# Gate logits with column tiles over quarters of the tokens, and VectorE's transpose to put them on token rows

## The chip, the cores and the metric

The kernel runs on one core of one Trainium2 chip. The metric is the device time of one execution in microseconds. The kernel before takes 374.43 us, the median of three runs (373.29 to 374.58).

Five engines matter: TensorE multiplies matrices (PE in the profile, PEld its weight loads), VectorE (DVE) and ScalarE (ACT) work on elements, GpSimd (POOL) adds tiles and issues the large loads, and SyncE (SP) issues transfers. SBUF is the working memory of 128 partitions; PSUM is the memory that TensorE writes.

## The reference, cut to what matters

An attention is followed by a mixture of experts with a gate in two stages. The gate is what the change touches: for each of 3072 tokens (8 batches of 384), 4 group logits and 4 expert logits of the chosen group.

```python
q: (8, 16, 384, 64)   k, v: (8, 4, 384, 64)
x = attention(q, k, v)                     # 3072 tokens x 1024
g_logits = x @ w_group                     # 1024 x 4
g_idx = argmax(g_logits)                   # and its softmax weight g_w
e_logits = x[g_idx == g] @ w_expert[g]     # 1024 x 4 for each of 4 groups
e_idx = argmax(e_logits)                   # and its softmax weight e_w
h  = maximum(x @ w1[g, e], 0)              # 1024 x 1024
ye = h @ w2[g, e]                          # 1024 x 1024
out = (g_w * e_w) * ye
```

The kernel computes all 4 + 16 = 20 logits of every token in one product with a matrix `wg` of 20 columns, padded to 32.

## The kernel before

It goes batch by batch; a "block" is one batch `b`, with its attention followed by the experts' products of the batch before it. The weights of one expert per batch are fetched early, by a guess: the mean of the next batch's `v` is put through the gate before its attention is done.

The parts that matter (`KQ` = 8 pieces of 128 of the 1024 features, `S` = 384 tokens, `SC` = 3 pieces of 128 tokens, `NW` = 20 logits; cuts are marked with `...`):

```python
def ps_tile(which, ...):        # PSUM: two tiles of two banks "s", two "o", taken in turn;
    ...                         # "x" is the "o" tile that is not the current one

# gate logits: 4 column tiles of 32 columns; each sums its own 2 of the 8 feature pieces
def gate_logits(b, pt):
    lg = pt[:, 0]
    for jj in range(KQ // 4):
        for t in range(4):
            kq = 4 * jj + t
            nc.tensor.matmul(out=lg[32 * t:32 * t + 32, :S], lhsT=wg[:, kq, :],
                             rhs=xT[b][:, kq, :],
                             start=(jj == 0), stop=(jj == KQ // 4 - 1))
    ls = gpool.tile([P, S], F32, name="lgs")
    nc.scalar.copy(out=ls, in_=lg[:, :S])
    lgs[b] = ls

# sums the four partial logits (mod32 has ones where row % 32 == column), tokens come to rows
def gate_tokens(b, glp):
    for c in range(SC):
        nc.tensor.matmul(out=glp[:, c, :], lhsT=lgs[b][:, c * P:(c + 1) * P],
                         rhs=mod32[:, 0, :NW], start=True, stop=True)

def guess_mean(b, pt): ...      # 12 small matmuls: mean of v, into pt[:, 1, :4]
def guess_logits(vm, glp): ...  # 4 small matmuls: the guess's logits, beside the tokens' logits

def gate_softmax(b, glp, guess, eng=None):
    ...
    evac(eng or nc.vector, gl, glp[:, lo:hi])      # one copy out of PSUM
    ...                                            # 9 small VectorE operations: both argmaxes

# the experts' products
def ffn_h(x, w1, hT, f0, which, mid=None):   # w1, two of eight pieces; then ReLU on ScalarE
    ...
def ffn_y(w2, hT, c, which, nhs=(0, 1), y=None, fs=None):   # w2, one of three token pieces
    ...

def block(b):
    f = b - 1
    prefetch(b)      # GpSimd: waits for the next batch's transposed q, then fetches w1, w2
    moe_h(f, 0, "s")
    ...
    sums(b, 0, Hkv, "o")
    for m in range(4):
        normalise(b, m)                      # xT, the gate's input
    ...
    moe_y(f, 0, "s")
    ...
    y = ffn_y(w2s[f], hTs[f], 1, "s", (0,))
    gate_logits(b, ps_tile("o"))
    ffn_y(w2s[f], hTs[f], 1, "s", (1,), y)
    y_out(f, 1, y)
    pt = ps_tile("s")
    glp = gate_rows(pt)
    gate_tokens(b, glp)
    if not last:
        guess_mean(b + 1, pt)
        vm = mean_copy(pt, nc.vector)
    y = ffn_y(w2s[f], hTs[f], 2, "o", (0,))
    if not last:
        guess_logits(vm, glp)
    weights[b] = gate_softmax(b, glp, not last)
    if not last:
        pick_index(b + 1)
        at[b + 1] = Attn(b + 1)
        y_scores(f, at[b + 1], y)            # rest of the third output piece, first scores
        return {}
    ...

def prefetch(b):
    if b != 2:
        pick(b)
    if b + 1 < B:
        transposed(b + 1)                    # GpSimd reads one column of the transposed q
    pick_w1(b)                               # 2 MB as bf16, cast on the way
    pick_w2(b)                               # the same
    if b + 2 < B:
        loads(b + 2)                         # v, k and q of the batch after the next
```

After the last block TensorE does the eighth batch's `ffn_h` (all of w1) and `ffn_y` (all of w2), and the results are written out. Blocks 0 and 1 have the same steps in a schedule of their own.

Of the kernel before, what the change touches and what calls it, by code (L numbers as in the profile page):

```python
# [9 lines left out]
F32 = mybir.dt.float32  # L10
# [8 lines left out]
def kernel(  # L19
# [416 lines left out]

    lgs = {}

    def gate_logits(b, pt):
        lg = pt[:, 0]
        for jj in range(KQ // 4):
            for t in range(4):
                kq = 4 * jj + t
                nc.tensor.matmul(out=lg[32 * t:32 * t + 32, :S], lhsT=wg[:, kq, :],  # L446
                                 rhs=xT[b][:, kq, :],
                                 start=(jj == 0), stop=(jj == KQ // 4 - 1))
        ls = gpool.tile([P, S], F32, name="lgs")
        nc.scalar.copy(out=ls, in_=lg[:, :S])  # L450
        lgs[b] = ls

    def guess_mean(b, pt):

# [13 lines left out]
    def gate_rows(pt):  # L468
        return pt[:, 1, 64:64 + (SC + 1) * NW].rearrange("p (c n) -> p c n", n=NW)

    def gate_tokens(b, glp):
        for c in range(SC):
            nc.tensor.matmul(out=glp[:, c, :], lhsT=lgs[b][:, c * P:(c + 1) * P],  # L473
                             rhs=mod32[:, 0, :NW], start=True, stop=True)

    def guess_logits(vm, glp):
        for g in range(Hkv):
            nc.tensor.matmul(out=glp[:, SC, :], lhsT=vm[:, g:g + 1].to_broadcast([P, P]),  # L478
                             rhs=wgd[:, g, :], start=(g == 0), stop=(g == Hkv - 1))

    def gate_softmax(b, glp, guess, eng=None):

        lo = 0 if b is not None else SC
        hi = SC + 1 if guess else SC
        n, nt = hi - lo, SC - lo
        gl = gpool.tile([P, SC + 1, NW], F32, name="gl")[:, lo:hi]
        evac(eng or nc.vector, gl, glp[:, lo:hi])
        mx = gpool.tile([P, 2, SC + 1], F32, name="mx")[:, :, lo:hi]
        nc.vector.tensor_reduce(out=mx[:, 0, :], in_=gl[:, :, :G], axis=AX.X, op=ALU.max)
        sh = gpool.tile([P, 2, SC + 1, G], F32, name="sh")[:, :, lo:hi]  # L490
# [3 lines left out]
        ohg = gpool.tile([P, SC + 1, G], F32, name="ohg")[:, lo:hi]  # L494
        nc.vector.tensor_single_scalar(ohg, sh[:, 0], 0.0, op=ALU.is_ge)
        pr = gpool.tile([P, SC + 1, G, Eg], F32, name="pr")[:, lo:hi]
        nc.vector.tensor_tensor(out=pr, in0=gl[:, :, G:].rearrange("p c (g e) -> p c g e", g=G),
                                in1=ohg.unsqueeze(3).to_broadcast([P, n, G, Eg]), op=ALU.mult)
        el = gpool.tile([P, SC + 1, Eg], F32, name="el")[:, lo:hi]
# [6 lines left out]
        ohe = gpool.tile([P, SC + 1, Eg], F32, name="ohe")[:, lo:hi]  # L506
        nc.vector.tensor_single_scalar(ohe, sh[:, 1], 0.0, op=ALU.is_ge)
        oh = oh_all[:, b, lo:hi] if b is not None else oh_first.unsqueeze(1)
        nc.vector.tensor_tensor(out=oh.rearrange("p c (g e) -> p c g e", g=G),
                                in0=ohg.unsqueeze(3).to_broadcast([P, n, G, Eg]),  # L510
                                in1=ohe.unsqueeze(2).to_broadcast([P, n, G, Eg]), op=ALU.mult)

        def weights():
            ex = gpool.tile([P, 2, SC, G], F32, name="ex")
            nc.scalar.activation(ex, sh[:, :, :nt], ACT.Exp)
# [9 lines left out]
    def first_choice(glp):  # L525

        gl = glp[:, SC, :]
# [155 lines left out]
        state["vm"] = mean_copy(state["pt"], nc.scalar)  # L683

    def first_pick():
        glp = gate_rows(state["pt"])
        guess_logits(state["vm"], glp)
        first_choice(glp)
        pick_index(0)

    def first_fetch():
# [61 lines left out]
    guess_mean(1, pt)  # L753
    vm = mean_copy(pt, nc.scalar)
    moe_h(0, 2, "s", do(sums, 1, 0, 2, "s"))
    glp = gate_rows(pt)
    gate_tokens(0, glp)
    guess_logits(vm, glp)
    for m in range(2):
        normalise(1, m)  # L760
    moe_h(0, 4, "s")
    weights[0] = gate_softmax(0, glp, True, nc.scalar)
    pick_index(1)
    moe_h(0, 6, "s")
    nc.sync.dma_start(out=xb_dram[0], in_=xb[0])
# [2 lines left out]
    def first_block():  # L768

        prefetch(1)  # L770
        collect(1, 2, Hkv)
        weights[0]()
        out_weights(0)
        cast(1, 0)
        cast(1, 1)
        moe_y(0, 0, "s")
        sums(1, 2, Hkv, "o")
        normalise(1, 2)
        normalise(1, 3)
        moe_y(0, 1, "s")  # L780
        cast(1, 2)
        cast(1, 3)
        nc.sync.dma_start(out=xb_dram[1], in_=xb[1])
        y = ffn_y(w2s[0], hTs[0], 2, "o", (0,))
        gt = ps_tile("x")
        guess_mean(2, gt)
        gate_logits(1, gt)
        state["vm"] = mean_copy(gt, nc.vector)
        at[2] = Attn(2)

        def second_gate():
            glp = gate_rows(gt)
            gate_tokens(1, glp)
            guess_logits(state["vm"], glp)
            weights[1] = gate_softmax(1, glp, True)
            pick_index(2)
            pick(2)

        y_scores(0, at[2], y, second_gate)
        return {}  # L800

# [10 lines left out]
    def block(b):  # L812
# [17 lines left out]
        cast(b, 3)  # L830
        nc.sync.dma_start(out=xb_dram[b], in_=xb[b])
        y = ffn_y(w2s[f], hTs[f], 1, "s", (0,))
        gate_logits(b, ps_tile("o"))
        ffn_y(w2s[f], hTs[f], 1, "s", (1,), y)
        y_out(f, 1, y)
        pt = ps_tile("s")
        glp = gate_rows(pt)
        gate_tokens(b, glp)
        if not last:
            guess_mean(b + 1, pt)  # L840
            vm = mean_copy(pt, nc.vector)
# [133 lines left out]
```

The softmax here doesn't subtract the row's maximum and nothing guards it: scores larger than these inputs give would overflow.

## Time and profile before

| | us |
|---|---|
| time, median of 3 | 374.43 |
| span of the profiled execution | 372.4 |
| TensorE busy | 361.1 |
| VectorE busy | 258.1 |
| ScalarE busy | 233.0 |
| GpSimd busy | 150.6 |

The lines that touch the gate, from the costliest groups with the shapes kept apart. The columns are: line, engine, operation, output <- inputs, shapes, count, then the busy time in us and the mean ns of one, then the engine's idle time before them and what ended it:

```profile
L446 PE MATMUL ps_o<-xT,wg 128*32 128x384 f32 x112 | 10.5, 492 | 0.0
...
L473 PEld LDWEIGHTS ps_s<-mod,lgs 128*128 128x128 f32 x36 | 5.0, 191 | 0.9
L473 PE MATMUL ps_s<-mod,lgs 128*128 128x20 f32 x36 | 4.4, 252 | 0.0
...
L450 ACT COPY lgs<-ps_o 128x384 f32<-128x384 f32 x8 | 3.8, 479 | 5.3 <-PE ps_o L446 5.3
```

L446 is `gate_logits`, L473 `gate_tokens`, L450 the copy between them, L460 `guess_mean`, L478 `guess_logits`, L305 and L324 the attention's two products, L611 `ffn_h`, L622 `ffn_y`. An fp32 matmul appears as two records, one for each pass. "128*32" is the part of the array that an instruction uses. The durations of matmuls overlap, so what one costs is read from where the next one starts, not from its own duration. A few matmul records are missing from the trace.

### The profile page before, as it was taken

The numbers are of one execution on the slowest core, as the hardware profiler recorded it, in microseconds if no ns is written. First come the engines' busy times: TensorE is split into PE (matmuls) and PEld (weight loads), VectorE is DVE, ScalarE is ACT, GpSimd is POOL, SyncE is SP. The second block draws the span as 40 slices with busy tenths as digits, with TensorE's granted clock in tenths as the row PEclk, the third lists the DMA queues.
The fourth block names the chain that finished last, engine by engine and source line by source line (L and its number), as shares of the span: only waits on it lengthen the run. The fifth ranks groups of instructions, "written<-read, shape, count | busy, mean of one in ns | idle before, by whom it ended". The sixth has DMA issues, their size and how long they took to land.

```text
span 372.4 us, 8914 instructions
## 1 busy us (share of the span) xinstructions
PE 361.1 (97%) x3648; PEld 183.8 (49%) x3663; DVE 258.1 (69%) x491; ACT 233.0 (63%) x309; POOL 150.6 (40%) x118
## 2 busy tenths in 40 slices
PE   8999999999999999999999999999999999999992
PEld 3545446445454545544555445544545445554641
DVE  5699787858976498737989189764897379892230
ACT  4789943759926597367954599265972679544221
POOL 6666950706804176033730367113760237500000
PEclk9999999999999999999999999999999999999997
DMA  8986999999999999999999999989999999999734
GB/s 189 242 108 101 241 213 156 234 239 281 222 152 184 249 263 210 147 195 291 238 208 153 255 246 216 199 167 246 264 212 150 203 212 238 196 201 234 238 73 99
DMA packets 71209, 76.02 MB, mean 204 GB/s; under 512 B 35928, under 2 KB 50264, under 8 KB 71168
## 3 DMA queue, kind: packets, MB, share of 16 engines
q0 software_dynamic: 26640, 41.03, 63.0%
q1 hardware_dynamic: 44096, 33.81, 37.1%
q8 instruction: 29, 0.48, 0.5%
q10 hardware_dynamic: 432, 0.61, 0.5%
q14 instruction: 12, 0.10, 0.1%
HBM read 89.21 MB, written 18.87 MB: 290 GB/s over the span
## 4 chain that ended last, share of the span: by engine, by line
PE 91%; DVE 3%; ACT 2%; issue 1%; POOL 1%; ACTq 0%; POOLq 0%
PE ps_o L324 29%; PE ps_s L611 21%; PE ps_s L622 14%; PE ps_s L305 8%; PE ps_o L622 8%; PE ps_o L446 3%; PE ps_o L268 2%; DVE red L338 1%; PE ps_o L611 1%; PE ps_o L408 1%; ACT e L311 1%; PE ps_s L473 1%; DVE ps_o L419 1%; DVE xT L428 1%; POOL e L331 1%
## 5 line engine op out<-in xcount | busy, mean ns | idle before, releaser
L311 ACT ACTIVATE e<-ps_s 128x768 f32<-128x768 f32 x192 | 150.3, 814 | 22.1 <-PE ps_s L305 19.3
L324 PE MATMUL ps_o<-e,v_raw 64*64 64x384 f32 x1536 | 153.1, 482 | 0.2 <-DVE xT L428 0.2
L331 POOL TENSOR_TENSOR e<-e 128x768 f32<-128x768 f32 x64 | 116.1, 1832 | 88.6 <-ACT e L311 64.6
L338 DVE TRANSPOSE_TENSOR_REDUCE red<-e 128x24 f32<-128x768 f32 x128 | 114.3, 947 | 11.9 <-POOL e L331 11.9
L611 PE MATMUL ps_s<-xb,w 128*128 128x384 bf16 x480 | 81.1, 326 | 0.4 <-ACT hT L615 0.2
L324 PEld LDWEIGHTS ps_o<-e,v_raw 64*64 64x64 f32 x1536 | 55.4, 133 | 37.5 <-issue 27.1
L611 PEld LDWEIGHTS <-w 128*128 128x128 bf16 x512 | 48.9, 98 | 36.1 <-issue 3.9
L305 PE MATMUL ps_s<-qT,kT 64*64 64x384 bf16 x768 | 63.7, 326 | 0.4 <-ACT e L311 0.2
L615 ACT ACTIVATE hT<-ps_s 128x768 bf16<-128x768 f32 x30 | 24.3, 810 | 61.0 <-PE ps_s L611 61.0
L622 PEld LDWEIGHTS <-hT 128*128 128x128 bf16 x384 | 35.5, 98 | 45.1 <-issue 6.5
L622 PE MATMUL ps_s<-w,hT 128*128 128x512 bf16 x240 | 56.0, 379 | 0.4
L305 PEld LDWEIGHTS <-kT 64*64 64x64 bf16 x768 | 24.3, 105 | 38.4 <-issue 36.7
L678 POOL COPY after<-qT 128x1 bf16<-128x1 bf16 x7 | 2.1, 301 | 79.8 <-DMA qT<-q_raw 76.9
L622 PE MATMUL ps_o<-w,hT 128*128 128x512 bf16 x129 | 31.1, 379 | 0.6 <-issue 0.2
L419 DVE STREAM_TRANSPOSE rb<-inv 128x384 f32<-128x384 f32 x60 | 31.0, 555 | 0.3
L647 ACT ACTIVATE ot<-ps_s,we 128x1024 f32<-128x1024 f32 x14 | 15.6, 1114 | 19.1 <-PE ps_s L622 19.1
L428 DVE TENSOR_TENSOR xT<-xT,rb 128x768 f32<-128x768 f32 x25 | 24.0, 958 | 0.9
L242 DVE CAST vm<-ps_s 128x4 bf16<-128x4 f32 x5 | 0.8, 163 | 29.8 <-PE ps_s L460 29.8
L240 ACT CAST xb<-xT 128x768 bf16<-128x768 f32 x27 | 21.1, 827 | 0.0
L374 DVE COPY xT<-ps_o 128x768 f32<-128x768 f32 x18 | 16.5, 919 | 0.0
L376 ACT COPY xT<-ps_o 128x768 f32<-128x768 f32 x10 | 8.0, 801 | 6.5 <-PE ps_o L324 6.5
L242 DVE COPY gl<-ps_s 128x80 f32<-128x80 f32 (+1 forms) x6 | 1.4, 239 | 14.0 <-PE ps_s L478 8.4
(132 smaller groups left out, 196.8 us busy)
## 6 DMA issues: line engine op xcount, KB each, us to landing
w<-in_moe_w_dram POOLq DMA_DIRECT2D x16, 2048.0 KB, 21.8
out_dram<-ot SPq DMA_DIRECT2D x42, 256.0 KB, 7.1
xb_scratch<-xb SPq DMA_DIRECT2D x8, 768.0 KB, 9.6
q_raw<-in_q_dram POOLq DMA_DIRECT2D x7, 768.0 KB, 33.7
v_raw<-in_v_dram SPq DMA_DIRECT2D x14, 384.0 KB, 5.6
out_dram<-ot SPq DMA_DIRECT2D x11, 128.0 KB, 2.3
k<-in_k_dram POOLq DMA_DIRECT2D x7, 192.0 KB, 30.5
w<-in_q_dram POOLq DMA_DIRECT2D x3, 192.0 KB, 6.7
```

The lines of the kernel that those rows point to most:

```text
L240: eng.copy(out=out_, in_=in_)
L305: nc.tensor.matmul(out=sT[r * H2:(r + 1) * H2, s, :S], lhsT=kT[b][s * D:(s + 1) * D, slot, ks], rhs=qT[b][s * D:(s + 1) * D, kq * SC:(kq + ...
L311: nc.scalar.activation(e.rearrange("p t (s x) -> p s t x", s=2), sT[:, :, :S].rearrange("p s (t x) -> p s t x", t=2), ACT.Exp, scale=scale)
L324: nc.tensor.matmul(out=oT[t * D:(t + 1) * D, r, :S], lhsT=vraw[b][r * H2:(r + 1) * H2, g, c * D:(c + 1) * D], rhs=self.e[u][r * H2:(r + 1) ...
L331: eng.tensor_add(out=self.e[u], in0=self.e[u], in1=self.e[u + 1])
L338: nc.vector.tensor_reduce(out=reds[self.b][:, g, n].rearrange("p t j -> p (t j)"), in_=self.e[u].rearrange("p t (j x) -> p (t j) x", x=32) ...
L374: nc.vector.tensor_copy(out=dst, in_=src)
L419: nc.vector.transpose(out=rb[:, r].rearrange("p (j x) -> p j x", x=32), in_=inv[b][:, 2 * m + r].unsqueeze(2).to_broadcast([P, NB, 32]))
L428: eng.tensor_mul(out=x, in0=x, in1=rb)
L611: nc.tensor.matmul(out=h[:, jj, :S], lhsT=w1[:, kq, (f0 + jj) * P:(f0 + jj + 1) * P], rhs=x[:, kq, :], start=(kq == 0), stop=(kq == KQ - 1))
L615: nc.scalar.activation(hT[:, f0:f0 + 2, :], h[:, :, :S], ACT.Relu)
L622: nc.tensor.matmul(out=y[:, nh, :], lhsT=hT[:, f, c * P:(c + 1) * P], rhs=w2[:, f, nh * HALF:(nh + 1) * HALF], start=(f == 0), stop=(f == ...
```

## The change

Before, the four column tiles split the features: each sums a quarter of x, for all tokens, and a second product on TensorE adds the four parts and turns the result so that tokens lie on rows. After, the four column tiles split the tokens: column tile `t` takes tokens 32t to 32t + 31 of each piece of 128, and sums all of x in place, in PSUM. The second product and the copy before it are no longer needed. VectorE's transpose of 32x32 blocks turns each block where it stands, which puts every token on its own row. It aims at less work on TensorE and ScalarE in each block, and one PSUM tile less.

The logits are now 32 matmuls of 96 columns instead of 8 of 384, and the small products of the guess move up: `guess_mean` right behind the logits, in the same PSUM tile, `guess_logits` and the softmax ahead of the third output piece. The core of the diff (cut: the softmax's views for a case that no longer occurs, and renamed arguments):

```diff
     def gate_logits(b, pt):
-        lg = pt[:, 0]
-        for jj in range(KQ // 4):
+        for kq in range(KQ):
+            x = xT[b][:, kq, :].rearrange("p (c t i) -> p t c i", t=4, i=32)
             for t in range(4):
-                kq = 4 * jj + t
-                nc.tensor.matmul(out=lg[32 * t:32 * t + 32, :S], lhsT=wg[:, kq, :],
-                                 rhs=xT[b][:, kq, :],
-                                 start=(jj == 0), stop=(jj == KQ // 4 - 1))
-        ls = gpool.tile([P, S], F32, name="lgs")
-        nc.scalar.copy(out=ls, in_=lg[:, :S])
-        lgs[b] = ls
+                nc.tensor.matmul(out=pt[32 * t:32 * t + 32, 0, :32 * SC], lhsT=wg[:, kq, :],
+                                 rhs=x[:, t], start=(kq == 0), stop=(kq == KQ - 1))
-    def gate_tokens(b, glp):
-        for c in range(SC):
-            nc.tensor.matmul(out=glp[:, c, :], lhsT=lgs[b][:, c * P:(c + 1) * P],
-                             rhs=mod32[:, 0, :NW], start=True, stop=True)
...
     def gate_softmax(b, pt, guess):
-        evac(eng or nc.vector, gl, glp[:, lo:hi])
+        gl = gpool.tile([P, SC + 1, 32], F32, name="gl")
+        nc.vector.transpose(out=gl[:, :SC], in_=pt[:, 0, :32 * SC].rearrange("p (c i) -> p c i", i=32))
+        if guess:
+            nc.vector.tensor_copy(out=gl[:, SC, :NW], in_=guess_row(pt))
...
 # block 0
-    glp = gate_rows(pt)
-    gate_tokens(0, glp)
-    guess_logits(vm, glp)
+    guess_logits(vm, pt)
...
 # block 1
         gt = ps_tile("x")
+        gate_logits(1, gt)
         guess_mean(2, gt)
-        gate_logits(1, gt)
         state["vm"] = mean_copy(gt, nc.vector)
...
 # blocks 2 to 7
-        gate_logits(b, ps_tile("o"))
-        ffn_y(w2s[f], hTs[f], 1, "s", (1,), y)
-        y_out(f, 1, y)
-        pt = ps_tile("s")
-        glp = gate_rows(pt)
-        gate_tokens(b, glp)
+        pt = ps_tile("o")
+        gate_logits(b, pt)
         if not last:
             guess_mean(b + 1, pt)
             vm = mean_copy(pt, nc.vector)
+        ffn_y(w2s[f], hTs[f], 1, "s", (1,), y)
+        y_out(f, 1, y)
+        if not last:
+            guess_logits(vm, pt)
+        weights[b] = gate_softmax(b, pt, not last)
         y = ffn_y(w2s[f], hTs[f], 2, "o", (0,))
-        if not last:
-            guess_logits(vm, glp)
-        weights[b] = gate_softmax(b, glp, not last)
```

More of the change, by code (lines that the diff above doesn't have):

```diff
@@ L435, in cast @@
         evac(eng or nc.scalar, xb[b][:, ks, :], xT[b][:, ks, :])
-    lgs = {}
     def gate_logits(b, pt):
-        lg = pt[:, 0]
-        for jj in range(KQ // 4):
+        for kq in range(KQ):
+            x = xT[b][:, kq, :].rearrange("p (c t i) -> p t c i", t=4, i=32)
             for t in range(4):
-                kq = 4 * jj + t
-                nc.tensor.matmul(out=lg[32 * t:32 * t + 32, :S], lhsT=wg[:, kq, :],
-                                 rhs=xT[b][:, kq, :],
-                                 start=(jj == 0), stop=(jj == KQ // 4 - 1))
-        ls = gpool.tile([P, S], F32, name="lgs")
-        nc.scalar.copy(out=ls, in_=lg[:, :S])
-        lgs[b] = ls
+                nc.tensor.matmul(out=pt[32 * t:32 * t + 32, 0, :32 * SC], lhsT=wg[:, kq, :],
+                                 rhs=x[:, t], start=(kq == 0), stop=(kq == KQ - 1))
     def guess_mean(b, pt):
@@ L466, in mean_copy, with guess_row, guess_logits, gate_softmax @@
         return vm
-    def gate_rows(pt):
-        return pt[:, 1, 64:64 + (SC + 1) * NW].rearrange("p (c n) -> p c n", n=NW)
-    def gate_tokens(b, glp):
-        for c in range(SC):
-            nc.tensor.matmul(out=glp[:, c, :], lhsT=lgs[b][:, c * P:(c + 1) * P],
-                             rhs=mod32[:, 0, :NW], start=True, stop=True)
-    def guess_logits(vm, glp):
+    def guess_row(pt):
+        return pt[:, 1, 64:64 + NW]
+    def guess_logits(vm, pt):
         for g in range(Hkv):
-            nc.tensor.matmul(out=glp[:, SC, :], lhsT=vm[:, g:g + 1].to_broadcast([P, P]),
+            nc.tensor.matmul(out=guess_row(pt), lhsT=vm[:, g:g + 1].to_broadcast([P, P]),
                              rhs=wgd[:, g, :], start=(g == 0), stop=(g == Hkv - 1))
[L481 to L486, printed above, removed]
-        evac(eng or nc.vector, gl, glp[:, lo:hi])
-        mx = gpool.tile([P, 2, SC + 1], F32, name="mx")[:, :, lo:hi]
+    def gate_softmax(b, pt, guess):
+        n = SC + 1 if guess else SC
+        gl = gpool.tile([P, SC + 1, 32], F32, name="gl")
+        nc.vector.transpose(out=gl[:, :SC], in_=pt[:, 0, :32 * SC].rearrange("p (c i) -> p c i", i=32))
+        if guess:
+            nc.vector.tensor_copy(out=gl[:, SC, :NW], in_=guess_row(pt))
+        gl = gl[:, :n, :NW]
+        mx = gpool.tile([P, 2, SC + 1], F32, name="mx")[:, :, :n]
         nc.vector.tensor_reduce(out=mx[:, 0, :], in_=gl[:, :, :G], axis=AX.X, op=ALU.max)
-        sh = gpool.tile([P, 2, SC + 1, G], F32, name="sh")[:, :, lo:hi]
+        sh = gpool.tile([P, 2, SC + 1, G], F32, name="sh")[:, :, :n]
         nc.vector.tensor_tensor(out=sh[:, 0], in0=gl[:, :, :G],
@@ L493, in gate_softmax @@
                                 op=ALU.subtract)
-        ohg = gpool.tile([P, SC + 1, G], F32, name="ohg")[:, lo:hi]
+        ohg = gpool.tile([P, SC + 1, G], F32, name="ohg")[:, :n]
         nc.vector.tensor_single_scalar(ohg, sh[:, 0], 0.0, op=ALU.is_ge)
-        pr = gpool.tile([P, SC + 1, G, Eg], F32, name="pr")[:, lo:hi]
+        pr = gpool.tile([P, SC + 1, G, Eg], F32, name="pr")[:, :n]
         nc.vector.tensor_tensor(out=pr, in0=gl[:, :, G:].rearrange("p c (g e) -> p c g e", g=G),
                                 in1=ohg.unsqueeze(3).to_broadcast([P, n, G, Eg]), op=ALU.mult)
-        el = gpool.tile([P, SC + 1, Eg], F32, name="el")[:, lo:hi]
+        el = gpool.tile([P, SC + 1, Eg], F32, name="el")[:, :n]
         nc.vector.tensor_reduce(out=el, in_=pr.rearrange("p c g e -> p c e g"), axis=AX.X,
@@ L505, in gate_softmax @@
                                 op=ALU.subtract)
-        ohe = gpool.tile([P, SC + 1, Eg], F32, name="ohe")[:, lo:hi]
+        ohe = gpool.tile([P, SC + 1, Eg], F32, name="ohe")[:, :n]
         nc.vector.tensor_single_scalar(ohe, sh[:, 1], 0.0, op=ALU.is_ge)
-        oh = oh_all[:, b, lo:hi] if b is not None else oh_first.unsqueeze(1)
+        oh = oh_all[:, b, :n]
         nc.vector.tensor_tensor(out=oh.rearrange("p c (g e) -> p c g e", g=G),
@@ L514, in weights @@
             ex = gpool.tile([P, 2, SC, G], F32, name="ex")
-            nc.scalar.activation(ex, sh[:, :, :nt], ACT.Exp)
+            nc.scalar.activation(ex, sh[:, :, :SC], ACT.Exp)
             sm = gpool.tile([P, 2, SC], F32, name="smx")
@@ L523, in gate_softmax, with first_choice @@
         return weights
-    def first_choice(glp):
-        gl = glp[:, SC, :]
+    def first_choice(gl):
         mx = gpool.tile([P, 2], F32, name="fmx")
@@ L685, in first_pick @@
     def first_pick():
-        glp = gate_rows(state["pt"])
-        guess_logits(state["vm"], glp)
-        first_choice(glp)
+        guess_logits(state["vm"], state["pt"])
+        first_choice(guess_row(state["pt"]))
         pick_index(0)
@@ L761 @@
     moe_h(0, 4, "s")
-    weights[0] = gate_softmax(0, glp, True, nc.scalar)
+    weights[0] = gate_softmax(0, pt, True)
     pick_index(1)
@@ L791, in second_gate @@
         def second_gate():
[L792 to L795, printed above, removed]
+            guess_logits(state["vm"], gt)
+            weights[1] = gate_softmax(1, gt, True)
             pick_index(2)
```

## The prediction

> **What bounds the kernel now.** I read the page first, for the shares, then the chain of waits, then the timeline of one steady block, and last the landings of the weight fetches.
>
> ```profile
> PE 361.1 (97%) x3648; PEld 183.8 (49%) x3663; DVE 258.1 (69%) x491; ACT 233.0 (63%) x309; POOL 150.6 (40%) x118
> ...
> DMA  8986999999999999999999999989999999999734
> ...
> PE 91%; DVE 3%; ACT 2%; issue 1%; POOL 1%; ACTq 0%; POOLq 0%
> ```
>
> TensorE is busy for 97% of the span and 91% of the chain that ended last is its own work. So an instruction taken off VectorE or ScalarE is worth nothing by itself; what counts is time on TensorE. But the DMA row stands at 9 almost throughout, so a second resource runs close behind. That is the trap in this case.
>
> The timeline of a steady block (the third), TensorE's rows of the gate (columns: start in us, duration in us, engine, line, operation):
>
> ```profile
> 119.34 1.50 PE L446 MATMUL ps_o<-xT,wg 128*32 128x384 f32 x16
> ...
> 120.77 1.90 PE L622 MATMUL ps_s<-w,hT 128*128 128x512 bf16 x8
> ...
> 122.50 0.74 PE L473 MATMUL ps_s<-mod,lgs 128*128 128x20 f32 x6
> ...
> 123.09 0.44 PE L460 MATMUL ps_s<-onesb,v_raw 128*128 128x1 bf16 x12
> ```
>
> L446 is the logits product: 8 matmuls, seen as 16 records because an fp32 matmul is recorded as two passes. It keeps TensorE from 119.34 to 120.77, 1.43 us. L473 is the sum over column groups that also puts tokens on rows: 3 matmuls, 6 passes, and TensorE comes to L460 only 123.09 - 122.50 = 0.59 us later. Nothing here waits: the rows follow each other.
>
> Block 0 is different (the same view around 53 us):
>
> ```profile
> 53.42 0.44 PE L460 MATMUL ps_o<-onesb,v_raw 128*128 128x1 bf16 x12 [0.60 <-ACT lgs L450]
> ...
> 55.11 0.42 PE L408 MATMUL ps_s<-rsum,half 128*64 128x24 f32 x8
> ...
> 57.83 0.48 PE L611 MATMUL ps_s<-xb,w 128*128 128x384 bf16 x2 [0.23 <-ACT hT L615]
> ```
>
> There L460 stands idle for 0.60 us until ScalarE has copied the logits out of the PSUM tile they share. And the L611 at 57.83 waits for ScalarE's hT anyway, so the L473 just before it fills a hole.
>
> Last, the final fetch of w2 (line L555, from the instruction's own view), the wait that starts such fetches (from the list of waits), and its first reader at the end (from the timeline):
>
> ```profile
> L555 POOL DMA_DIRECT2D w<-in_moe_w_dram x1: 893/893/893, 322.1 to 322.1; - x1
> ...
> DMA to landing us min/median/max: 30.3/30.3/30.3
> ```
>
> ```profile
> POOL after L678 <- DMA qT<-q_raw: 76.9, 6, 17.4
> ```
>
> ```profile
> 355.12 1.89 PE L622 MATMUL ps_s<-w,hT 128*128 128x512 bf16 x7
> ```
>
> It lands at 322.1 + 30.3 = 352.4 us, and TensorE first needs it at 355.12. The slack is 2.7 us.
>
> **What the skill says.** The Trainium skill, "TensorEngine Tiling (Array Packing)", section Key Properties: tiles of the array load weights and multiply independently and in parallel, and a change of tiling mode drains the engine. The trace agrees; the weight loads of L446 in block 3, by the timeline:
>
> ```profile
> 119.33 0.16 PEld L446 LDWEIGHTS ps_o<-xT,wg 128*32 128x32 f32 x8 [0.42 <-issue]
> 119.68 0.13 PEld L446 LDWEIGHTS ps_o<-xT,wg 128*32 128x32 f32 x4 [0.19 <-issue]
> 120.01 0.13 PEld L446 LDWEIGHTS ps_o<-xT,wg 128*32 128x32 f32 x4 [0.19 <-issue]
> ```
>
> They come in fours, one four per round of matmuls, so four column tiles run together. The change has the same two changes of mode in each block.
>
> The skill, "TensorE: Matmul & The Clock Gate", section LDWEIGHTS: a load takes time by its columns, columns / 1.2 ns, so an estimate of 27 ns for 32. The trace's means for fp32 loads are 109 ns at 32 columns (L446), 136 at 64 (L408), 191 at 128 (L473), a slope of (191 - 109) / 96 = 0.85 ns per column: again 27 ns for 32 columns, above a fixed latency that overlaps.
>
> "VectorE: DVE Perf Modes", section The three transpose paths: VectorE transposes 32x32 blocks only. That is why the change gives each column tile one quarter of the tokens in each 128: the four 32x32 blocks of a 128-token piece then come out on their own token rows. No run yet shows this transpose from PSUM; L419 (128x384, 555 ns) is the nearest.
>
> "DMA: Bandwidth & Descriptors", section Issuing engines are not separate DMA queues: what SP, ACT and POOL start shares the same 16 engines. The DMA row agrees, and w2's landing says the same: 30.3 us for this fetch, in part behind and beside other transfers.
>
> **The change, part by part.**
>
> *Logits product.* Before: two rounds of four column tiles, two passes each, so 4 rounds of 384 columns, 120.01 - 119.68 = 0.33 us apart. After: 8 rounds of four, two passes each, so 16 rounds of 96 columns; 0.33 / 4 = 0.082 us each, 16 x 0.082 = 1.32 us, as before. That holds if 32-column loads hide behind 82 ns. L408 is my test: 8 passes on two column tiles with 64-column loads take 0.42 us with 24 moving columns (above) and 0.44 with 48 (block 3). Half the work, same time: there the load sets the pace, about (0.42 - 0.22) / 3 = 0.07 us at most for a round of two tiles, where 0.22 is one record's duration. A load of half the columns is well below 0.082. I add 0.03 us for the extra starts. The moving operand is now read in runs of 32 fp32, 128 bytes; the scores read qT in runs of 64 bf16, also 128 bytes, and their 384 columns take the same 326 ns as L611's contiguous ones. So no charge for it.
>
> *Token rows on TensorE (L473).* Gone: 0.59 us in each of blocks 2 to 7. In block 1 it stands from 82.03 to the next line at 82.73, 0.70 us. In block 0 it is worth nothing, for the reason above.
>
> *Copy of the logits on ScalarE (L450, 479 ns).* Gone. ScalarE is not on the path in blocks 1 to 7, so 0 there. In block 0 the 0.60 us wait of L460 goes with it.
>
> *Guess of the next block's expert.* L460 moves up behind the logits product and L478 before the third output chunk; their cost (0.30 and 0.10 us) is unchanged. L478 has 8 matmuls of L622 (1.7 us) between it and L460 for VectorE's small cast (163 ns).
>
> *VectorE.* In place of one copy (242 ns) come a transpose of 128x96 (estimate 0.25 to 0.3 us, from 555 ns at 384 columns and about 0.16 for the smallest operations) and a copy of 128x20 (0.17). That is 0.2 us more in each block on an engine that is idle at that point, and the chain starts some 2.5 us earlier. Not on the path.
>
> *PSUM.* The separate score-type tile for the token rows is gone, so the first scores of the next block take other buffers. They wait for ScalarE's output scaling, done more than a microsecond earlier. No charge.
>
> Sum on TensorE: block 0: 0.60 - 0.03 = 0.57; block 1: 0.70 - 0.03 = 0.67; blocks 2 to 7: 6 x (0.59 - 0.03) = 3.36. Together **4.6 us** by the time TensorE asks for the last w2.
>
> *What that meets.* TensorE would want w2 at 355.1 - 4.6 = 350.5. It lands at 352.4, unless the transfers speed up too, and I see no reason for that: each fetch is issued once the next block's q is transposed, which is a DMA in its turn (the 76.9 us of POOL's waits), not when TensorE gets there. The bytes to be moved before it are the same. So TensorE waits about 1.9 us, and 2.7 of the 4.6 remain. From w2 to the end nothing changes. 374.4 - 2.7 = **371.7 us**.
>
> **The rivals.**
>
> 1. *The full gain.* The transfers are not rigid: output writes come earlier and w2 lands earlier with them. For: it shares its last microseconds with writes of the outputs. Against: those only change places. Time 374.4 - 4.6 = 369.8. I give it a quarter.
> 2. *The small matmuls cost more.* If the four loads of a round ran one after another, a round would take 4 x 27 = 108 ns instead of 82: 16 x 26 = 0.4 us more per block. Then the sum is 4.6 - 8 x 0.4 = 1.4, and the time 373.0. Against: in block 3 eight loads of L446 are recorded within 0.16 us. About one in seven.
> 3. *An earlier collision.* Block 6's w1 is fetched at 295.7, lands 20.1 us later at 315.8, and is first read at 321.2: a slack of 5.4 us now, and savings of up to 4 us run towards it. If earlier output writes push into the q transposes, the fetch chain slips by up to 1 us, and w2 with it: 372.7. One in ten.
> 4. *A loss.* VectorE's longer chain could hold up the PSUM tile or the reductions. It starts 2.5 us earlier, so I see no way; a few per cent.
>
> **Range and chances.** The main line gives 371.7, pulled down a little by the full gain and up by rivals 2 and 3: 371.6. 369.9 to 373.2 covers the first two rivals nearly. Over 2% faster would be below 366.9, past the whole TensorE saving: 3%. Over 2% slower would be above 381.9: 2%. Within 2%: 95%.
>
> **What would show it.** In the profile after: L473's group and the L450 copy gone; the logits product between neighbours in about 1.45 us (rival 2: 1.85); TensorE's last block earlier by 4 to 5 us up to the last hidden layer; then a wait of 1 to 2 us of the first L622 on the DMA of w2, landing within 1 us of 352.4. If that wait is missing and the end is 4 us earlier, the claim that transfers are rigid was wrong. If the blocks are not 0.55 us shorter each, the cost of the logits product was.

## The result, and the profile after

The changed kernel takes **369.35 us** (median of 4 executions, 368.97 to 371.23), the kernel before in the same comparison 373.99 us. The ratio is 0.9884, with a 95% interval of 0.9850 to 0.9919: 1.2% faster, 4.6 us. The prediction was 371.6 us with a range of 369.9 to 373.2. So the gain is larger than predicted, and equals the whole saving on TensorE, which the prediction had named as its first rival and given a quarter.

The profiled execution differs from the other three: it took 371.23 us, the longest of the four. Its page, first the busy time of TensorE and of the DMA engines in 40 slices, then the chain that ended last:

```profile
PE 357.0 (97%) x3984; PEld 185.7 (50%) x3999; DVE 259.2 (70%) x499; ACT 228.7 (62%) x300; POOL 150.0 (41%) x118
...
DMA  8995999999999999999999999989999899999834
...
PE 81%; DMA 9%; DVE 4%; ACT 2%; issue 1%; POOL 1%; POOLq 0%; ACTq 0%
```

Before, 91% of that chain was TensorE's own work and no DMA was in it. Now 9% is a DMA. TensorE's rows of block 2, by the timeline (start, duration, engine, line, operation), against L446, L473 and L460 of before:

```profile
118.36 1.53 PE L444 MATMUL ps_o<-xT,wg 128*32 128x96 f32 x64
119.82 0.45 PE L454 MATMUL ps_o<-onesb,v_raw 128*128 128x1 bf16 x12
120.35 1.67 PE L611 MATMUL ps_s<-w,hT 128*128 128x512 bf16 x7
121.86 0.25 PE L467 MATMUL ps_o<-wgd,vm 128*128 128x20 bf16 x4
```

The logits product is now L444. It holds TensorE for 119.82 - 118.36 = 1.46 us, before 1.43. The token product between the output pieces is gone. And the end of the last block, the same view:

```profile
350.62 0.38 PE L849 MATMUL ps_o<-oh_all,onesb 128*128 128x512 bf16 x1
352.17 1.02 PE L611 MATMUL ps_s<-w,hT 128*128 128x512 bf16 x3 [1.17 <-DMA w<-in_moe_w_dram]
```

L849 (L867 before) is followed 0.22 us later by the first reader of the last w2 when nothing is in the way. Here it would have started at 350.84 and starts at 352.17, behind the DMA of w2: 1.33 us of waiting. That is the predicted picture: TensorE 4.3 us earlier, w2 landing at 352.1, a wait of 1 to 2 us. But most executions do not show it.

### The profile page after: what moved, and what is told of

It is laid out like the page before. It is cut to its first block, busy times and chain, and to the rows that moved or that the text cites. A ratio compares the mean times of both kernels' runs of the same rounds, so it can differ in the third digit from the quotient of the medians.

```text
span 369.5 us, 9587 instructions
## 1 busy us (share of the span) xinstructions
PE 357.0 (97%) x3984; PEld 185.7 (50%) x3999; DVE 259.2 (70%) x499; ACT 228.7 (62%) x300; POOL 150.0 (41%) x118
## 4 chain that ended last, share of the span: by engine, by line
PE 81%; DMA 9%; DVE 4%; ACT 2%; issue 1%; POOL 1%; POOLq 0%; ACTq 0%
PE ps_o L324 28%; PE ps_s L600 17%; PE ps_s L611 13%; DMA w<-in_moe_w_dram 9%; PE ps_s L305 8%; PE ps_o L611 7%; PE ps_o L444 3%; PE ps_o L268 2%; DVE red L338 1%; POOL e L331 1%; ACT e L311 1%; PE ps_o L408 1%; PE ps_o L454 1%; DVE ps_o L419 1%; DVE xT L428 1%
## 5 line engine op out<-in xcount | busy, mean ns | idle before, releaser
L331 POOL TENSOR_TENSOR e<-e 128x768 f32<-128x768 f32 x64 | 116.1, 1831 | 78.6 <-ACT e L311 54.4
L305 PE MATMUL ps_s<-qT,kT 64*64 64x384 bf16 x768 | 63.7, 326 | 0.4 <-ACT e L311 0.2
L604 ACT ACTIVATE hT<-ps_s 128x768 bf16<-128x768 f32 x30 | 24.3, 810 | 62.0 <-PE ps_s L600 62.0
L611 PEld LDWEIGHTS <-hT 128*128 128x128 bf16 x384 | 36.0, 98 | 43.6 <-issue 3.6
L611 PE MATMUL ps_s<-w,hT 128*128 128x512 bf16 x234 | 54.6, 379 | 2.1 <-DMA w<-in_moe_w_dram 1.2
L305 PEld LDWEIGHTS <-kT 64*64 64x64 bf16 x768 | 24.4, 105 | 38.4 <-issue 36.7
L667 POOL COPY after<-qT 128x1 bf16<-128x1 bf16 x7 | 1.3, 192 | 86.4 <-DMA qT<-q_raw 83.5
L636 ACT ACTIVATE ot<-ps_s,we 128x1024 f32<-128x1024 f32 x14 | 15.6, 1114 | 27.3 <-PE ps_s L611 27.3
L611 PE MATMUL ps_o<-w,hT 128*128 128x512 bf16 x135 | 31.9, 379 | 0.1
L242 DVE CAST vm<-ps_o 128x4 bf16<-128x4 f32 x6 | 1.0, 161 | 21.0 <-PE ps_o L454 21.0
L638 DVE TENSOR_SCALAR ot<-ps_o,we 128x1024 f32<-128x1024 f32 x7 | 9.0, 1282 | 5.3 <-PE ps_o L611 5.1
```

Of the source, the lines that this page charges most:

```text
L305: nc.tensor.matmul(out=sT[r * H2:(r + 1) * H2, s, :S], lhsT=kT[b][s * D:(s + 1) * D, slot, ks], rhs=qT[b][s * D:(s + 1) * D, kq * SC:(kq + ...
L331: eng.tensor_add(out=self.e[u], in0=self.e[u], in1=self.e[u + 1])
L604: nc.scalar.activation(hT[:, f0:f0 + 2, :], h[:, :, :S], ACT.Relu)
L611: nc.tensor.matmul(out=y[:, nh, :], lhsT=hT[:, f, c * P:(c + 1) * P], rhs=w2[:, f, nh * HALF:(nh + 1) * HALF], start=(f == 0), stop=(f == ...
```

## The experiments

The block period on TensorE, read from one start of the logits product to the next, is the same in every profile of one kernel to 0.01 us: 43.59 us before and 43.04 after. So TensorE's share was settled from the start. The question was when the last w2 lands, and why the timed executions are shorter than the profiled one.

In what follows "wanted" is the start of L849 plus 0.22 us, and "landed" the landing of the last w2's fetch.

**Is w2 waited for in ordinary executions?** Four runs, compared with the kernel before on the same chip.

The changed kernel once more, without an edit.

> The changed kernel once more. In its profiled execution TensorE waited about 1.3 us for the last w2 (landing at 352.1), and took 371.2 us; the three timed executions took 369.0 to 369.6. Theory A (the profile slows the transfers, or meets a bad one: in ordinary executions w2 lands before it is wanted): timed executions again near 369.3, the profiled one longer by 1 us or more and with the wait. Theory B (transfers simply differ from one execution to the next, in the profiled ones as in the others): timed executions spread over 368.9 to 371.5, and the profile may show no wait this time. Theory C (the wait is in every execution, and the timed ones gain elsewhere, in the first 50 us): timed near 369.3, profile with the wait.

369.51 us (369.34 to 370.02), ratio 0.9887 (0.9871 to 0.9903). This time the profile shows no wait:

```profile
350.11 0.38 PE L849 MATMUL ps_o<-oh_all,onesb 128*128 128x512 bf16 x1
350.33 1.89 PE L611 MATMUL ps_s<-w,hT 128*128 128x512 bf16 x7
```

And the fetch, in the view of its own line:

```profile
L544 POOL DMA_DIRECT2D w<-in_moe_w_dram x1: 883/883/883, 317.9 to 317.9; - x1
...
DMA to landing us min/median/max: 31.9/31.9/31.9
```

It landed at 317.9 + 31.9 = 349.8, before it was wanted. In the first profile the same view has 318.4 + 33.7 = 352.1. TensorE's pace does not differ: the last batch's hidden layer starts 291.3 us after the first batch's in both.

The filler on TensorE, seven matmuls whose result nobody reads:

```diff
+    warm = ps_tile("o")
+    for i in range(7):
+        nc.tensor.matmul(out=warm[:, i % 2, :], lhsT=onesb[:, :P], rhs=onesb, start=True,
+                         stop=True)
     for f0 in range(0, FQ, 2):
         moe_h(B - 1, f0, "so"[(f0 // 2) % 2])
```

> The changed kernel with 7 idle matmuls of 512 columns (1.51 us of TensorE) ahead of the last batch's hidden layer, so TensorE asks for the last w2 1.51 us later. If w2 is waited for in ordinary executions too (rival, theory C), the filler fits into the wait: at most 0.2 us longer than the changed kernel. If it is not waited for there (theory A), 1.5 us longer. Between the two: the mean wait in ordinary executions is 1.5 less the measured difference. In the profiled execution, if w2 lands near 352 as before, no or little wait and a span within 0.3 us of 369.5.

371.01 us, ratio 0.9920 (0.9904 to 0.9936): 1.50 us more than the run before it. The filler's 1.51 us counts in full, so there was no wait for it to fit into.

The last product with a w2 that is there anyway:

```diff
-            ffn_y(w2s[B - 1], hTs[B - 1], c, "", (nh,), y)
+            ffn_y(w2s[B - 2], hTs[B - 1], c, "", (nh,), y)
```

> The changed kernel with the last output product reading the w2 of the batch before (it leaves out nothing of the work, but the last batch's output is computed with another expert's w2); the last w2 is still fetched, so the traffic is the same. Theory C: 1.3 us shorter than the changed kernel, in timed executions too. Theory A: timed executions the same within 0.3 us, the profiled one about 1.3 us shorter than 369.5, with a span near 368.2.

369.62 us, ratio 0.9884 (0.9866 to 0.9903): no shorter. From both sides the same answer: in timed executions of the changed kernel w2 is there in time.

The scratch write of the last batch moved behind w2:

```diff
-        nc.sync.dma_start(out=xb_dram[b], in_=xb[b])
+        if not last:
+            nc.sync.dma_start(out=xb_dram[b], in_=xb[b])
...
+        if c == 0:
+            nc.sync.dma_start(out=xb_dram[B - 1], in_=xb[B - 1])
```

> The changed kernel with the last batch's 768 KB scratch write moved from before the last w2 has landed to after the first output piece of the last batch. It takes 0.77 MB out of the traffic that w2's last 2 MB share. If transfers before w2 are what sets its landing, w2 lands 2 to 4 us earlier and the wait in the profiled execution is gone (span near 368.2). Theory A: timed executions unchanged within 0.3 us; theory C: 1.3 us shorter.

369.84 us, ratio 0.9886 (0.9870 to 0.9903). In its one profile w2 landed at 345.8 and was wanted at 351.0; that is earlier than in any profile with the full traffic (347.7 to 352.1, below). The time does not move, as w2 was not waited for.

**Does the landing differ from one execution to the next, or with the change?** Two more profiles of the kernel before, one of the changed kernel.

> The kernel before once more, for the landing of its last w2. In its first profile it landed at 352.4 us, and the prediction took that as fixed; four executions of the changed kernel or of variants with the same traffic had it at 352.1, 349.8, 347.7 and 350.2. Theory D (the transfers do not follow TensorE, but differ by some microseconds from one execution to the next, and the first two profiles were both late ones): this kernel lands it somewhere between 347 and 352.5 as well, and not always at 352. Theory E (the rival of the prediction: with less work on TensorE the output writes move earlier and the transfers end earlier): here it lands at 352 to 353 again.

> As the run before it, a second draw. Theory D: between 347 and 352.5, differing from the other by a microsecond or more. Theory E: 352 to 353 both times.

> The changed kernel a third time, for the same question: theory D: w2 lands between 347 and 352.5, and TensorE waits for it only if it lands after about 350.4. Theory E: near 350, always earlier than in the kernel before.

| execution profiled | w2 wanted, us | landed, us | wait, us |
|---|---|---|---|
| before | 355.1 | 352.4 | - |
| before, r5 | 355.3 | 353.4 | - |
| before, r6 | 354.2 | 352.5 | - |
| changed | 350.8 | 352.1 | 1.3 |
| changed, r1 | 350.3 | 349.8 | - |
| changed, r7 | 349.8 | 351.3 | 1.5 |
| changed with filler, r2 | 351.8 | 347.7 | - |
| changed, other w2 read, r3 | 350.8 | 350.2 | not read |

Both theories, D and E, hold a part. With the change the landing differs by more than 4 us between executions (347.7 to 352.1), and TensorE waits in those where it is late. r7 is one, with 370.62 us; its timeline:

```profile
349.62 0.38 PE L849 MATMUL ps_o<-oh_all,onesb 128*128 128x512 bf16 x1
351.33 1.02 PE L611 MATMUL ps_s<-w,hT 128*128 128x512 bf16 x4 [1.33 <-DMA w<-in_moe_w_dram]
```

L611 stands 1.7 us behind L849, where r1 has 0.22. Yet the three of the kernel before lie together and later, at 352.4 to 353.4.

**Is the saving on TensorE what the sum says?** The token product put back, its result unused:

```diff
+    def gate_tokens(b, pt):
+        for c in range(SC):
+            nc.tensor.matmul(out=pt[:, 1, 128 + 32 * c:128 + 32 * c + NW],
+                             lhsT=xT[b][:, 0, c * P:(c + 1) * P],
+                             rhs=mod32[:, 0, :NW], start=True, stop=True)
...
+        gate_tokens(b, pt)               # in each block, before guess_logits
```

> The changed kernel with three fp32 matmuls of 128x128 weights and 20 columns put back into each block where the kernel before had them (their result is not used). By the prediction's sum they cost 0.59 us in each of blocks 2 to 7, 0.70 in block 1 and nothing in block 0, 4.2 us together: 369.5 + 4.2 = 373.7 us, within 0.7 us of the kernel before. Rival: part of the gain came from elsewhere (the scores' other PSUM buffers, ScalarE's copy gone): then it is at most 372.5. If block 0 is not free for them: 374.3.

373.77 us, ratio 0.9994 (0.9983 to 1.0004), against 373.7 expected. Its block period is 43.62 us. So the token product is worth 43.62 - 43.04 = 0.58 us a block, and nothing else in the change moves a block by more than 0.03.

**Can the hole in block 0 be closed?** In the changed kernel TensorE waits there for ScalarE's hidden layer, where the token product stood:

```profile
56.41 0.25 PE L467 MATMUL ps_o<-wgd,vm 128*128 128x20 bf16 x4
57.48 0.81 PE L600 MATMUL ps_s<-xb,w 128*128 128x384 bf16 x4 [0.81 <-ACT hT L604]
```

The sums take a scores tile there, so the next pair of hidden pieces has to wait for the other one. On top of the late scratch write:

```diff
-    moe_h(0, 2, "s", do(sums, 1, 0, 2, "s"))
+    sm = pt[:, 1, 128:128 + Hkv * KG * NB].rearrange("p (g r j) -> p g r j", g=Hkv, r=KG)
+    moe_h(0, 2, "s", do(sums, 1, 0, 2, "s", sm))      # sums() writes to sm if given
```

> The changed kernel with the late scratch write and, in block 0, the sums of the next batch put into the free part of the gate's PSUM tile in place of a scores tile of their own. The hidden layer's third pair of pieces then need not wait for ScalarE: in the changed kernel TensorE stands still for about 0.9 us there, a hole that the token product used to fill in part. If the hole is on the path: 0.8 us shorter than the changed kernel, 368.6 to 368.9, and no wait for w2. Rival: the attention that follows is held by ScalarE and VectorE, and gives the 0.8 us back: no change, 369.5.

369.02 us, ratio 0.9868 (0.9851 to 0.9884). The timeline, with its lines one further on:

```profile
56.81 0.25 PE L468 MATMUL ps_o<-wgd,vm 128*128 128x20 bf16 x4
56.92 3.25 PE L601 MATMUL ps_s<-xb,w 128*128 128x384 bf16 x19
```

The hole is gone. The profile reaches L849 300.8 us after the first hidden layer's start, in r1 and r4 301.7. The time gains 0.5 us on r1 and 0.8 us on r4, which has the same late scratch write; both intervals overlap with its own, so this is the fastest version tried, not one that is shown to beat the change.

**Do four column tiles need to stand side by side?** The two loops of the logits product exchanged:

```diff
-        for kq in range(KQ):
-            for t in range(4):
+        for t in range(4):
+            for kq in range(KQ):
```

> The changed kernel with the two loops of the logits product exchanged: all eight feature pieces of one column tile, then the next tile. The work is the same. If four tiles run at once only when their matmuls stand next to each other (weight loads and matmuls are started in order), each pass takes 0.08 us alone: 64 x 0.08 = 5.1 us instead of 1.35, so 3.8 us more per block, 30 us in all: near 399 us. If TensorE starts ready tiles out of order, nothing changes: 369.5.

393.73 us, ratio 1.0532 (1.0514 to 1.0549), 24.2 us more than r1. The timeline of block 2 again:

```profile
124.56 4.57 PE L444 MATMUL ps_o<-xT,wg 128*32 128x96 f32 x64
129.06 0.45 PE L454 MATMUL ps_o<-onesb,v_raw 128*128 128x1 bf16 x12
```

The same 64 passes now take 4.50 us in place of 1.46: 3.04 more in each of eight blocks make 24.3. Within a column tile the passes start 0.082 us apart, as far apart as the rounds of four were; 64 of them would take 5.3. Only where one tile ends and the next begins do the starts stand closer (0.006 to 0.076 us).

**What moves the landing?** To see it in timed executions, TensorE must always wait for w2. The last hidden layer is cut to 2 of 8 feature pieces (it leaves out three quarters of that product):

```diff
-        moe_h(B - 1, f0, "so"[(f0 // 2) % 2])
+        moe_h(B - 1, f0, "so"[(f0 // 2) % 2], nk=2)
```

> The changed kernel with only 2 of 8 feature pieces in the hidden layer of the last batch (it leaves out three quarters of that product; nothing of the traffic). TensorE then asks for the last w2 some 6 to 7 us earlier, near 344 us, and waits for it in every execution. From w2's landing to the end of the measured time it is 19.2 us (371.23 - 352.13, 370.62 - 351.29), so the time is the landing plus 19.2: timed executions show when w2 lands without looking at a trace. Theory A (transfers are slower in a profiled execution): timed executions put the landing 2 us or more before that of the profiled one. Theory D (only differences between executions): timed and profiled landings spread over the same 347.5 to 352, the mean near 350: times of 367 to 371. If w2 landed near 345 in timed executions: 364.

> The same cut in the kernel before: TensorE asks for the last w2 near 348.5. Theory E (the transfers end earlier when TensorE's work is shorter): landings of 352 to 353.5 as in its three profiles, times of 371.2 to 372.7, some 2 to 3 us above the cut of the changed kernel. Theory D alone: the same landings, and the same times within 1 us, as with the changed kernel.

The cut of the changed kernel took 370.92 us (ratio 0.9909, 0.9889 to 0.9929), that of the kernel before 373.71 (0.9983, 0.9967 to 0.9998). Both wait for w2, here by the timeline, the changed one first:

```profile
343.16 0.38 PE L849 MATMUL ps_o<-oh_all,onesb 128*128 128x512 bf16 x1
349.69 3.57 PE L611 MATMUL ps_s<-w,hT 128*128 128x512 bf16 x8 [6.16 <-DMA w<-in_moe_w_dram]
```

```profile
346.55 0.38 PE L867 MATMUL ps_o<-oh_all,onesb 128*128 128x512 bf16 x1
352.71 3.57 PE L622 MATMUL ps_s<-w,hT 128*128 128x512 bf16 x8 [5.79 <-DMA w<-in_moe_w_dram]
```

Both times are the landing plus some 21 us (371.52 - 349.65 = 21.9 and 374.12 - 352.67 = 21.5; 20.5 to 21.9 over the seven kernels with the cut), not 19.2 as expected: after so long a wait the first matmuls run slowly. Three things follow. With the cut the changed kernel is 2.8 us faster, and the intervals are apart; so the landing is earlier, by about as much (the way from landing to end differs by up to 1.4 us between these profiles). It spreads: the single times of the cut kernel before run from 370.66 to 375.20, where the uncut one has 373.06 to 374.99 over all its runs. And the profile is no slower than other executions: in r12 its 374.12 lies inside that spread, and in r11 its 371.52 is 0.8 above the median of the other five (370.72), where Theory A asked for 2 or more. Theory A falls.

Then the pace and the place of TensorE, each with the cut: the token product put back (the edit of r8), and 21 matmuls whose result nobody reads (4.5 us) once at the start of block 2, beside the cut of the changed kernel again.

```diff
         prefetch(b)
+        if b == 2:
+            warm = ps_tile("o")
+            for i in range(21):
+                nc.tensor.matmul(out=warm[:, i % 2, :], lhsT=onesb[:, :P], rhs=onesb,
+                                 start=True, stop=True)
         moe_h(f, 0, "s")
```

> The changed kernel with the three token matmuls of each block put back (TensorE's old pace, everything else of the change), and the cut of the last hidden layer to 2 of 8 feature pieces. If w2's landing follows TensorE's pace: as with the cut of the kernel before, 373 to 374.5 us. If it comes from the other parts of the change (no copy on ScalarE, other PSUM tiles, VectorE earlier): as with the cut of the changed kernel, 370.5 to 371.5.

> The changed kernel with the cut of the last hidden layer, and 21 idle matmuls (4.5 us of TensorE) once, at the start of block 2. From there on every output write comes 4.5 us later than in the cut of the changed kernel, at the changed kernel's pace. If the landing depends on where the writes stand against the fetches: 2 to 4 us later, 373 to 375 us. If only the pace per block counts, or the transfers do not depend on TensorE: within 1 us of the cut of the changed kernel, 370 to 372.

> The cut of the changed kernel again, on the same chip as the two: 370.9 as the first time if the chip does not matter; it is what the two are compared with.

| with the cut | us | ratio (95%) |
|---|---|---|
| changed kernel, r15 | 369.36 | 0.9879 (0.9856 to 0.9902) |
| token product back, r13 | 370.86 | 0.9919 (0.9894 to 0.9945) |
| 4.5 us of filler at block 2, r14 | 373.61 | 0.9979 (0.9962 to 0.9996) |

The same cut took 370.92 as r11, so only runs made together on one chip are compared. The token product, which by the traces of r8 and the changed kernel delays block 2 by 0.7 and block 7 by 3.6 us, moves the time by 1.5; its interval overlaps that of r15. A delay of 4.5 us from block 2 on moves it by 4.2. So the transfers are not rigid: they end later when TensorE is later, though the fetches up to block 6 are issued when a transposed q has landed and not when TensorE gets there.

The output and scratch writes do wait for its results. In the last two runs they are taken from the w1 tile in place of the results (same bytes, same order of issue; the output is not the reference's):

```diff
-            nc.sync.dma_start(out=out_rows(out[b * S:(b + 1) * S])[x], in_=ot[ps])
+            nc.sync.dma_start(out=out_rows(out[b * S:(b + 1) * S])[x],
+                              in_=w1s[b].rearrange("p a n -> p (a n)").bitcast(F32)[ps, :DM])
```

and the scratch write likewise.

> The cut of the changed kernel with all output and scratch writes of the blocks taken from the w1 tile, which has landed some microseconds before, in place of the results (same bytes, same order of issue, no wait for TensorE; the output is left wrong). The transfers now depend on each other alone. Landing within 3 us of the cut of the changed kernel, 367 to 372 us; it is what the next run is compared with.

> The same with the 21 idle matmuls (4.5 us) at the start of block 2. If the writes are what ties the landing to TensorE: within 1 us of the run before it, where the same delay made 4.2 us with writes that wait for results. If something else ties it (the loads of v, or GpSimd's queue): 3 to 4.5 us more than the run before it.

371.78 us, ratio 0.9935 (0.9912 to 0.9959), and with the delay 0.9937 (0.9916 to 0.9958). By the ratios the delay of 4.5 us no longer counts. But the executions of r17 spread from 368.5 to 378.0 us, the ratio leaves the eight longest of the twenty out, and the median of all is 373.2, 1.4 above r16.

This pair does not test the link as it was meant to. The edit also moved the fetches: the w2 of block 6 lands some 10 us later than in r15 (273.2 there; table below), and TensorE now waits for it, 3.9 us in r16 and 0.5 in r17. The last block takes 48.98 us in r16 and 43.90 in r17 in place of 43.04, so the delay is used up before the last product: L849 starts 299.9 and 299.3 us after the first hidden layer.

**What the traces say of the last fetch.** The prediction tied every fetch to the transposed q of the next block. The last pair has no next block: `prefetch` waits only `if b + 1 < B`. On GpSimd this pair stands right behind the last additions of the attention (L331), which wait for scores from TensorE (L305). In the kernel before (L549 fetches w1):

```profile
317.69 3.60 POOL L331 TENSOR_TENSOR e<-e 128x768 f32<-128x768 f32 x2 [1.24 <-PE ps_s L305]
321.22 0.92 POOL L549 DMA_DIRECT2D w<-in_moe_w_dram  x1
```

and in the changed one (L538 fetches w1):

```profile
313.95 3.60 POOL L331 TENSOR_TENSOR e<-e 128x768 f32<-128x768 f32 x2 [1.23 <-PE ps_s L305]
317.51 0.92 POOL L538 DMA_DIRECT2D w<-in_moe_w_dram  x1
```

The first hidden layer starts between 47.7 and 49.6 us, depending on the execution. Counted from there, in us, over the profiles with the full traffic:

| profiles | block 6's w2 landed | last w2 issued | last w2 landed | from landing to landing |
|---|---|---|---|---|
| before, r5, r6, r12 | 277.4 to 278.5 | 273.5 | 303.8 to 304.7 | 26.3 to 27.3 |
| changed, r1, r2, r3, r7, r11, r15 | 272.9 to 277.7 | 269.5 | 299.2 to 303.4 | 25.7 to 27.1 |
| token product back, r8, r13 | 275.6, 276.0 | 273.1 | 302.7, 301.8 | 27.1, 25.8 |
| 4.5 us of filler, r14 | 277.4 | 274.0 | 305.0 | 27.6 |
| free writes, r16 | 283.6 | 269.5 | 303.2 | 19.6 |
| free writes and filler, r17 | 284.7 | 274.0 | 304.5 | 19.7 |

So the last w2 is issued at TensorE's pace, the same to 0.03 us in all profiles of a row, and 4.0 us earlier with the change. Yet that alone does not set its landing. Without the freed writes it lands 25.7 to 27.6 us behind block 6's w2, whether it is issued at 269.5 or at 274.0. Most of the gain is there already at block 6, whose fetch does wait for a q: its w2 lands at 277.9 in the mean of the four profiles of the first row and at 275.1 in the seven of the second, 2.8 of the 3.3 us by which the means of the last w2 differ. What moves that earlier part of the chain was not found; the output writes are one candidate, and no run moves them alone.

## Why the prediction was right or wrong

- *TensorE bounds the kernel, and only its time counts*: right. The copy on ScalarE and the longer chain on VectorE left no trace in the block period. The two new VectorE operations, from the groups:

```profile
L474 DVE STREAM_TRANSPOSE gl<-ps_o 128x96 f32<-128x96 f32 x8 | 2.3, 282 | 12.8 <-PE ps_o L467 9.5 <-PE ps_o L444 3.3
...
L476 DVE COPY gl<-ps_o 128x20 f32<-128x20 f32 x7 | 1.0, 139 | 0.0
```

  282 and 139 ns, against 0.25 to 0.3 and 0.17 us expected, and VectorE was idle before them.
- *The logits product costs 0.03 us more*: right, 1.46 against 1.43 us. The timeline of its weight loads in block 2:

```profile
118.36 1.31 PEld L444 LDWEIGHTS ps_o<-xT,wg 128*32 128x32 f32 x64 [0.42 <-issue]
```

  All 64 lie within 1.31 us, a round of four each 0.082 us, which is the matmuls' own pace: they hide. Rival 2 falls; r10 shows what it costs when the four do not stand side by side.
- *The token product is worth 0.59 us in blocks 2 to 7*: right; the blocks are 43.59 - 43.04 = 0.55 us shorter, and 0.58 come back with it (r8).
- *Block 0 gives the wait for ScalarE's copy, 0.57, and nothing for the token product; block 1 0.67*: right within the reading. From block 0's logits to block 2's takes 66.77 us against 68.01, 1.24 less, which is the sum of the two.
- *Sum of 4.6 us*: right. In the first profiles the last hidden layer starts 4.54 us earlier, counted from block 0's logits product (344.50 - 51.33 and 340.22 - 51.59).
- *"It lands at 352.4, unless the transfers speed up too, and I see no reason for that"*: **this step failed.** It made one profile's landing a constant, and the wait of 1.9 us came from it. The slack of 2.7 us was itself one draw: r5 and r6 have 1.8 and 1.7. In the changed kernel w2 lands earlier, by about 2.8 us in the timed executions with the cut, and its landing differs by some 4 us between executions. Wanted at about 350.4, it is usually there: the filler of r2 found no wait to fit into. So TensorE's 4.6 us come through whole, where the prediction took 1.9 away. Of its two reasons, "each fetch is issued once the next block's q is transposed" does not hold for the fetch it was used for, which TensorE's pace releases; "the bytes to be moved before it are the same" is true and did not keep the landing in place.
- *Rival 1, the full gain*: this is what happened. Its ground, that output writes come earlier and w2 lands earlier with them, is not shown. In r14, where everything TensorE releases comes 4.5 us later, the time moves by 4.2; but the writes and the last fetch move there together.
- *Rival 3, an earlier collision that makes the chain slip*: did not happen. In the first profile block 6's w1 lands at 315.4 and is first read at 317.41, and the chain came earlier, not later.
- *Rival 4, a loss through VectorE's longer chain*: did not happen; no block became longer.
- *What would show it*: the prediction asked for a wait of 1 to 2 us on w2's DMA, landing within 1 us of 352.4. The first profile has just that (1.33 us, 352.1), so that profile alone would have borne the prediction out, and r7 looks the same (1.5 us, 351.3). The profile of r1 and the timed executions contradict it.

What stays open: why the chain of fetches up to block 6 runs earlier in the changed kernel. r14 shows that delaying TensorE moves the end of the chain; whether through the output writes was not shown (r16 and r17 changed more than the link). Which part of the 2.8 us belongs to the pace in each block (r13: 1.5, with overlapping intervals) was not settled either.

## What to carry to other kernels

A slack read from one profile is one draw: if a predicted gain is to end at a transfer, look at the landing in several executions, and move the wait on purpose (a filler before it, a cut before it) to see it in timed ones. Before a transfer is called independent of the compute, look at what releases that very transfer: here the fetches up to block 6 waited for a DMA, and the last, on which the prediction rested, did not. Its landing came about 2.8 us earlier with the same bytes to move. And with column tiles, loop over the tiles inside and the contraction outside: the order alone was worth 3 us a product here.

## What the runs showed of the hardware that was not expected

After the waits of some 5 to 6 us in the cut kernels, TensorE came back at about half speed. In r11 the first 8 matmuls of 512 columns take from 349.69 until the next tile's begin at 353.06, 3.4 us, at a granted clock of 0.50; in the changed kernel they take 1.72 (352.17 to 353.89), at 1.00. The next 8 take 2.73 us in r11, at 0.63, in place of 1.73. So this wait cost some 2.7 us more than its length. After the wait of 1.3 us in the changed kernel nothing was lost.

The time at which the chain of large fetches ends varies by some 4 us from one execution to the next: in seven profiles of the changed kernel and of variants with the same traffic the last w2 landed 299.2 to 303.4 us after the first hidden layer's start, while TensorE's block period repeats within 0.01 us. As long as the last fetch is not waited for, the kernel's time hides that.
